# Nine instead of eight fc1 feature tiles run once per batch, in a diffusion transformer block

## The chip, the cores and the metric

The kernel runs on one core of one Trainium2 chip. The metric is the device time of one execution in microseconds (us), as the median of several executions. Every execution whose state is on record was fast, at a granted TensorE clock of 0.99 to 1.0. The rounds of runs were made on different chips, so each kernel is compared with runs of the kernel before from the same round. Times inside one execution are read from the hardware profile and count from the start of its span. Engines are PE (TensorE matmuls), PEld (its weight loads), DVE (VectorE), ACT (ScalarE), POOL (GpSimd) and SP (SyncE, which issues most DMAs here).

## The reference

```python
B, N, D = 2, 256, 1152;  F = 4 * D;  H = 2          # all data bf16
mod = (silu(c) @ w_mod).reshape(B, 6, 1, D)          # shift, scale, gate for both halves
h = layernorm(x) * (1 + scale_a) + shift_a
... attention with two heads of 576, output projection wo ...
x = x + gate_a * a
h2 = layernorm(x) * (1 + scale_m) + shift_m          # the second LayerNorm
m = gelu(h2 @ w_fc1) @ w_fc2                         # fc1: 1152 -> 4608, fc2: 4608 -> 1152
return x + gate_m * m
```

## The kernel before

The argument is about one place, the seam in fc1 between batch 0 and batch 1. fc1 has KF = 36 feature tiles of 128, each summed over KD = 9 tiles of the input, and T = 512 tokens: 256 of batch 0 and 256 of batch 1. A matmul can stream all 512 tokens at once, but batch 1's second LayerNorm ends later than batch 0's. So the first eight feature tiles run twice with 256 tokens, first for batch 0 and then for batch 1, while batch 1's LayerNorm is still finishing. The other 28 tiles run with 512 tokens.

Token tiles 0 and 1 are batch 0's, 2 and 3 batch 1's. The normalized tokens of each are turned by a transposing DMA (`ln2_transpose`) into `hT`, where `ln2_modulate` applies scale and shift in place:

```python
    def ln2_transpose(t):
        nc.sync.dma_start_transpose(hT[:, :, t * P:(t + 1) * P], xn2[t][:])

    def ln2_modulate(b, ks=range(KD)):
        for k in ks:
            h = hT[:, k, b * N:(b + 1) * N]
            if b == 0 or k % 3 == 2:
                nc.scalar.activation(            # batch 1: k = 2, 5, 8 on ACT
                    h, h, ACT.Identity, bias=shift_m[:, k, b:b + 1], scale=scale_m[:, k, b:b + 1],
                )
            else:
                nc.vector.tensor_scalar(...)     # batch 1: k = 0, 1, 3, 4, 6, 7 on DVE
    ...
    ln2_normalize(3, 4 * P)
    ln2_transpose(3)                             # the fourth transpose: the last tile of batch 1
    w_f1[1] = load_panels("w_f1_1", wfc1_v, D)   # fc1's further weights, same DMA queue
    ...
    MSPLIT = 8
    for b in range(B):
        for m0 in range(0, MSPLIT, 2):
            pacc = acc_tile([P, 2, N], "pacc")
            for m in (m0, m0 + 1):
                for k in range(KD):
                    f1_mm(pacc[:, m - m0, :], m, k, b * N, (b + 1) * N)
            if b == 0 and m0 == MSPLIT - 2:
                ln2_modulate(1)                  # ahead of the GELU of tiles 6 and 7
            nc.scalar.activation(gT[:, m0:m0 + 2, b * N:(b + 1) * N], pacc[:], ACT.Gelu_apprx_tanh)
    ...
    for m in range(MSPLIT, KF):                  # 512 tokens from here on
```

At the very start, PE runs warm-up matmuls on zeros while the first weights load. The experiments use them:

```python
    def warm(n, dst):
        for _ in range(n):
            nc.tensor.matmul(dst[:], zeros[:, 0:P], zeros[:], start=True, stop=True)   # 512 columns, bf16
    warm(2, pwarm)
    ...
    warm(18, pwarm)
```

ACT runs the GELUs and the pieces of `ln2_modulate` in the order in which the program issues them.

## Time and profile before

| | |
|---|---|
| time, first three executions | 245.28 us (245.0 to 245.95) |
| span of the profiled execution | 243.1 us |
| PE busy | 237.1 us, 98% |
| fc1 (line 707), PE busy | 71.0 us |
| start of the first fc1 matmul to start of the first fc2 matmul | 70.79 us |

These lines are from the profile page of the kernel before: busy time per engine, the chain that ended last, and the costliest group (operation, shapes, count, busy us, mean ns, then idle time before it).

```profile
PE 237.1 (98%) x1652; PEld 139.4 (57%) x1652; DVE 83.7 (34%) x194; ACT 66.7 (27%) x130; POOL 31.3 (13%) x47
...
PE 93%; DMA 3%; DVE 1%; SPq 0%; ACT 0%; issue 0%; DVEq 0%
...
L707 PE MATMUL pacc<-hT,w_f 128*128 128x512 bf16 (+1 forms) x396 | 71.0, 340 | 0.0
```

PE is the bound, and fc1 seems to have no gap. The chain in order of time says the same about the seam (start us, length us, what):

```profile
98.56 7.86 PE pacc L707 x72
106.42 0.01 issue
106.42 62.93 PE pacc L707 x324
```

The 72 matmuls of batch 0 are followed by the rest with 0.01 us between. This is where a reader can be misled. The ends of matmuls are modelled and overlap the next start, so a matmul held for 0.15 us leaves no idle time. "Perfetto Trace Analysis" of the Trainium skill (Tensor Engine Instruction) says that the end the profiler reports for a matmul is an estimate computed from its size; this trace agrees, since consecutive 256-column matmuls start 0.109 us apart and are each recorded as 0.273 us long. The starts have to be compared. Those of the records around the seam, in us, with the step from the one before:

```
batch 0, tile 7, k = 8    106.147   0.109
batch 1, tile 0, k = 0    106.425   0.278
                 k = 1    106.683   0.258
                 k = 2    106.791   0.108
                 k = 3    106.938   0.147
                 k = 4    107.196   0.258
                 k = 5    107.304   0.108
                 k = 6    107.452   0.148
                 k = 7    107.708   0.256
                 k = 8    107.817   0.109
```

The steps over 0.109 us add up to 0.69 us lost. ACT's and DVE's timelines show what they follow (start us, length us, engine, line, operation, count, idle time before and what ended it):

```profile
106.01 1.58 ACT L595 ACTIVATE hT<-hT,shift_m,scale_m 128x256 bf16<-128x256 bf16 x3 [0.48 <-DMA hT<-xn]
107.50 0.57 ACT L722 ACTIVATE gT<-pacc 128x512 bf16<-128x512 f32 x1
...
106.03 1.63 DVE L599 TENSOR_SCALAR hT<-hT,scale_m,shift_m 128x256 bf16<-128x256 bf16 x6 [3.77 <-DMA hT<-xn]
```

Both engines idle until the transposing DMA lands, at 106.0 us. The six DVE pieces then take 1.63 us, and PE's matmuls follow them one by one.

### The profile page before, as it was taken

The numbers are of one execution on the slowest core, as the hardware profiler recorded it, in microseconds if no ns is written. First come the engines' busy times: TensorE is split into PE (matmuls) and PEld (weight loads), VectorE is DVE, ScalarE is ACT, GpSimd is POOL, SyncE is SP. The second block draws the span as 40 slices with busy tenths as digits, with TensorE's granted clock in tenths as the row PEclk, the third lists the DMA queues.
The fourth block names the chain that finished last, engine by engine and source line by source line (L and its number), as shares of the span: only waits on it lengthen the run. The fifth ranks groups of instructions, "written<-read, shape, count | busy, mean of one in ns | idle before, by whom it ended". The sixth has DMA issues, their size and how long they took to land.

```text
span 243.1 us, 3903 instructions
## 1 busy us (share of the span) xinstructions
PE 237.1 (98%) x1652; PEld 139.4 (57%) x1652; DVE 83.7 (34%) x194; ACT 66.7 (27%) x130; POOL 31.3 (13%) x47
## 2 busy tenths in 40 slices
PE   8899999999999999999999999999999999999994
PEld 2585444465656676978444444444665666656674
DVE  3752462115635676720000019999002000000001
ACT  7632250133614075773322222333000000000000
POOL 1000013000310615200000000000314211111111
PEclk9999999999999999999999999999999999999999
DMA  6999999999999992299999999999891000000000
GB/s 231 328 334 362 370 327 313 363 362 336 374 235 347 342 193 49 49 236 330 326 327 273 246 206 337 327 326 280 240 282 49 16 19 16 16 20 27 22 16 19
DMA packets 70813, 53.89 MB, mean 222 GB/s; under 512 B 18939, under 2 KB 65419, under 8 KB 70795
## 3 DMA queue, kind: packets, MB, share of 16 engines
q1 hardware_dynamic: 70064, 52.43, 74.1%
q0 software_dynamic: 704, 1.20, 1.8%
q8 instruction: 13, 0.21, 0.4%
q14 instruction: 5, 0.04, 0.1%
q10 hardware_dynamic: 27, 0.00, 0.0%
HBM read 48.08 MB, written 1.19 MB: 203 GB/s over the span
## 4 chain that ended last, share of the span: by engine, by line
PE 93%; DMA 3%; DVE 1%; SPq 0%; ACT 0%; issue 0%; DVEq 0%
PE pacc L707 29%; PE pacc L767 29%; PE pacc L612 7%; PE pacc L503 7%; PE pacc L438 7%; PE pk L253 4%; DMA w_scale_a<-in_w_mod_dram 3%; PE pk L282 2%; PE pn L365 1%; PE pa L530 1%; PE ps_s L458 1%; PE pm L221 1%; DVE stats L163 1%; PE pt L231 1%; PE pg L398 0%; SPq L85 0%
## 5 line engine op out<-in xcount | busy, mean ns | idle before, releaser
L707 PE MATMUL pacc<-hT,w_f 128*128 128x512 bf16 (+1 forms) x396 | 71.0, 340 | 0.0
L767 PE MATMUL pacc<-w_f,gT 128*128 128x384 bf16 (+2 forms) x468 | 70.5, 314 | 0.0
L767 PEld LDWEIGHTS <-gT 128*128 128x128 bf16 x468 | 44.3, 98 | 26.3
L707 PEld LDWEIGHTS <-w_f 128*128 128x128 bf16 x396 | 38.7, 98 | 31.9 <-issue 0.7
L429 DVE SCALAR_TENSOR_TENSOR late<-w_gate_mT,late 128x1152 bf16<-128x1152 bf16 x18 | 24.4, 1357 | 38.0 <-DMA w_gate_mT<-in_w_mod_dram 37.4
L773 DVE TENSOR_TENSOR tmp<-pacc,gate 128x384 f32<-128x384 f32 (+2 forms) x13 | 6.8, 526 | 62.6 <-PE pacc L767 50.3
L744 ACT ACTIVATE gT<-pacc 128x512 bf16<-128x512 f32 x28 | 16.7, 597 | 37.7 <-PE pacc L707 37.7
L612 PE MATMUL pacc<-w_o,big 128*128 128x384 bf16 (+2 forms) x117 | 18.1, 314 | 0.0
L503 PE MATMUL pacc<-w_v,hT 128*128 128x384 bf16 x108 | 17.9, 326 | 0.0
L775 POOL TENSOR_TENSOR o_sb<-tmp,x 128x384 bf16<-128x384 f32 (+1 forms) x12 | 11.6, 972 | 47.6 <-DVE tmp L773 47.6
L438 PE MATMUL pacc<-hT,w_q 128*128 128x512 bf16 x81 | 17.7, 379 | 0.0
L612 PEld LDWEIGHTS <-big 128*128 128x128 bf16 x117 | 10.9, 98 | 7.1 <-DVE big L270 0.6
L503 PEld LDWEIGHTS <-hT 128*128 128x128 bf16 x108 | 10.4, 98 | 7.2 <-issue 0.5
L253 PE MATMUL pk<-big,w_k 128*128 128x256 bf16 (+2 forms) x90 | 13.4, 294 | 0.4 <-ACT big L240 0.4
L438 PEld LDWEIGHTS <-w_q 128*128 128x128 bf16 x81 | 7.8, 98 | 9.8 <-DMA w_q<-in_wqkv_dram 0.5
L618 POOL TENSOR_TENSOR x<-tmp,x_sb 128x384 f32<-128x384 f32 (+1 forms) x11 | 9.8, 888 | 17.4 <-DVE tmp L617 10.7
L420 POOL DMA_DIRECT2D gates_dram<-grow x4 | 2.0, 512 | 71.4 <-DVE grow L730 71.4
L253 PEld LDWEIGHTS <-w_k 128*128 128x128 bf16 x90 | 7.5, 97 | 3.4 <-DMA w_k<-in_wqkv_dram 0.3
L146 PE MATMUL pwarm<-zeros 128*128 128x512 bf16 x23 | 7.7, 483 | 1.2 <-DVE eps_t L92 1.2
L617 DVE TENSOR_TENSOR tmp<-pacc,gate 128x384 f32<-128x384 f32 (+2 forms) x13 | 6.7, 525 | 5.4 <-PE pacc L612 5.3
L595 ACT ACTIVATE hT<-hT,shift_m,scale_m 128x256 bf16<-128x256 bf16 x12 | 6.2, 588 | 3.8 <-DVE stats L624 3.3
L240 ACT ACTIVATE big<-pt,scale_a 128x256 bf16<-128x256 bf16 (+1 forms) x12 | 4.6, 434 | 9.3 <-PE pt L231 7.6
(96 smaller groups left out, 146.8 us busy)
## 6 DMA issues: line engine op xcount, KB each, us to landing
w_f<-in_w_fc_dram SPq DMA_DIRECT2D x14, 864.0 KB, 10.9
w_f<-in_w_fc_dram SPq DMA_DIRECT2D x2, 2592.0 KB, 11.8
w_f<-in_w_fc_dram SPq DMA_DIRECT2D x2, 1728.0 KB, 14.9
w_shift_a<-in_w_mod_dram SPq DMA_DIRECT2D x3, 864.0 KB, 11.3
w_q<-in_wqkv_dram SPq DMA_DIRECT2D x3, 864.0 KB, 12.0
w_v<-in_wqkv_dram SPq DMA_DIRECT2D x3, 864.0 KB, 10.5
w_gate_a<-in_w_mod_dram SPq DMA_DIRECT2D x3, 864.0 KB, 9.9
w_o<-in_wo_dram SPq DMA_DIRECT2D x3, 864.0 KB, 13.8
```

The lines of the kernel that those rows point to most:

```text
L146: nc.tensor.matmul(dst[:], zeros[:, 0:P], zeros[:], start=True, stop=True)
L253: nc.tensor.matmul(pk[m][:, c0:c1], w_k[:, k, m * P:(m + 1) * P], hT0[:, k, c0:c1], start=(k == 0 and c0 == 0), stop=(k == KD - 1), skip_g ...
L429: nc.vector.scalar_tensor_tensor(spill, wT[:, j, :], 1.0, s_all[:, b, :], op0=ALU.mult, op1=ALU.mult, accum_out=dst[:, b * KD + j:b * KD + ...
L438: nc.tensor.matmul(pacc[:], w_q[:, k, m * P:(m + 1) * P], hT[:, k, :], start=(k == 0), stop=(k == KD - 1),)
L503: nc.tensor.matmul(pacc[:], hT[:, k, t * P:(t + 1) * P], w_v[:, k, pnl * PW:(pnl + 1) * PW], start=(k == 0), stop=(k == KD - 1),)
L612: nc.tensor.matmul(pacc[:], aT[:, k, t * P:(t + 1) * P], w_o[:, k, c0:c1], start=(k == 0), stop=(k == KD - 1),)
L618: (nc.vector if (t, i) in ((1, 2), (3, 3)) else nc.gpsimd).tensor_tensor(x1[:, t, c0:c1], tmp[:], x_sb[:, t, c0:c1], op=ALU.add)
L707: nc.tensor.matmul(dst, w_f1[m // KD][:, k, ml * P:(ml + 1) * P], hT[:, k, c0:c1], start=(k == 0), stop=(k == KD - 1),)
L744: nc.scalar.activation(gT[:, m, :], pacc[:], ACT.Gelu_apprx_tanh)
L767: nc.tensor.matmul(pacc[:], gT[:, kk, t * P:(t + 1) * P], w_f2[j][:, r, c0 - n * PW:c0 - n * PW + cw], start=(kk == 0), stop=(kk == KF - 1),)
L773: nc.vector.tensor_tensor(tmp[:], pacc[:], gate_m[:, b, c0:c0 + cw], op=ALU.mult)
L775: (nc.vector if last else nc.gpsimd).tensor_tensor(o_sb[:], tmp[:], x1[:, t, c0:c0 + cw], op=ALU.add)
```

## The change

The extra tile of batch 0 gives PE 9 matmuls (0.98 us) more to do before it needs batch 1's data. The first quarter of fc1's weights holds nine tiles, so nothing has to be loaded earlier. This is the whole diff:

```diff
-    MSPLIT = 8
+    MSPLIT = KD
     for b in range(B):
         for m0 in range(0, MSPLIT, 2):
-            pacc = acc_tile([P, 2, N], "pacc")
-            for m in (m0, m0 + 1):
+            ms = range(m0, min(m0 + 2, MSPLIT))
+            pacc = acc_tile([P, len(ms), N], "pacc")
+            for m in ms:
                 for k in range(KD):
                     f1_mm(pacc[:, m - m0, :], m, k, b * N, (b + 1) * N)
-            if b == 0 and m0 == MSPLIT - 2:
+            if b == 0 and ms[-1] == MSPLIT - 1:
                 ln2_modulate(1)
-            nc.scalar.activation(gT[:, m0:m0 + 2, b * N:(b + 1) * N], pacc[:], ACT.Gelu_apprx_tanh)
+            nc.scalar.activation(gT[:, ms[0]:ms[-1] + 1, b * N:(b + 1) * N], pacc[:], ACT.Gelu_apprx_tanh)
```

It has a side effect that the diff hardly shows: the call of `ln2_modulate(1)` moves one group later, so on ACT the GELU of tiles 6 and 7 now comes ahead of the three pieces k = 2, 5, 8.

## The prediction

> **What bounds the kernel now.** TensorE. The page gives PE 237.1 us busy, 98% of a 243.1 us span, at full granted clock; the chain of waits is 93% PE, with fc1 (line 707) 29% and fc2 (line 767) 29%. From the first fc1 matmul (98.40 us) to the end of fc2 (239.66 us) no PE idle time is charged. Only PE time in that stretch counts.
>
> **PE's work.** Feature tile 8 becomes 18 matmuls of 256 columns in place of 9 of 512. In the records, start to start is 109.15 ns for 256 columns and 215.83 ns for 512: 18 x 109.15 - 9 x 215.83 = +22 ns. The nine extra weight loads (98 ns each) still hide behind 109 ns matmuls.
>
> **The intent: the seam between batches.** Batch 1's fc1 needs the second LayerNorm's modulated columns of batch 1. Their transposing DMA lands at 106.01 us; PE issues batch 0's last matmul at 106.15. The modulation runs six pieces on DVE (pitch 0.257 us, from 106.03) and three on ACT (k = 2, 5, 8; pitch 0.50 us, from 106.01). The single matmul records show PE stretched here, though the page calls it busy: batch 1's first nine matmuls start at 106.43, 106.68, 106.79, 106.94, 107.20, 107.30, 107.45, 107.71, 107.82, where 109 ns steps would have put the last at 107.13. PE loses 0.69 us, each time released about 0.055 us after a DVE piece ended. The extra tile of batch 0 gives PE 9 x 0.109 = 0.98 us of work there, enough to hide the DVE pieces: a gain of up to 0.69 us (0.28%).
>
> **What takes it back.** The order listing shows that the three ACT pieces move behind one more GELU, that of tiles 6 and 7, because the call was tied to the last group. A GELU starts 0.42 us after the start of its last matmul, so at 106.57. The next ACT instruction follows 0.49 us later: k = 2 starts at 107.06, k = 5 at 107.56, k = 8 at 108.06, which ends (0.59 us long) at 108.65; its matmul can start at 108.70. PE, unheld, would want it at 107.24 + 8 x 0.109 = 108.11. So about 0.59 us of stall remains, on ACT in place of DVE. Before starts its 90th fc1 matmul at 108.80, after at 108.70: 0.10 us gained, less 0.02 of longer matmuls: -0.08 us in all.
>
> **The rest.** fc1's second quarter is in flight before the seam and nothing waits for it; the first fc2 load still waits for the same last use of the first quarter, and fc2 starts 50 us later. ACT idles over 1.3 us between GELUs, so two more cost nothing. "TensorE: Matmul & The Clock Gate" of the Trainium skill (Part 2) says that matmuls stay in program order and only weight loads are pulled ahead, so PE cannot fill a stall with later matmuls; the stretched starts agree.
>
> **Predicted time:** 245.2 us, range 244.6 to 245.9 (before spread 245.0 to 245.95). Faster by over 2%: 0.005; within 2%: 0.99; slower: 0.005.
>
> **What would show it.** After: k = 0 and 1 of batch 1's first tile unheld, starts at k = 2, 5, 8 held near 107.7, 108.2, 108.7, each just after an ACT piece; DVE pieces unmoved at 106.03; fc2 starting within 0.2 us of 169.35.
>
> **What would make it wrong.** ACT running the pieces earlier (gain up to 0.7 us), a later GELU (loss), or a shift between sessions larger than the effect.

## The result and the profile after

| | before | after |
|---|---|---|
| time, median of six | 245.45 us (244.97 to 246.12) | 246.12 us (245.65 to 246.45) |
| span of the profiled execution | 243.1 us | 244.3 us |
| start of the first fc1 matmul to start of the first fc2 matmul | 70.79 us | 71.64 us |
| issue of the fourth transpose to its landing | 3.26 us | 5.06 us |
| lost at the seam (steps over 0.109 us, added up) | 0.69 us | 1.52 us |

The two profiled spans differ by 1.2 us: 0.85 us of it is fc1, and 0.39 us is that fc1 starts later (98.79 us against 98.40). This start scatters between profiles of either kernel (98.48 us in a second profile of the changed kernel, 98.50 in one of the kernel before), so the duration of fc1 is the cleaner measure of the change.

The ratio is 1.0025, with a 95% interval from 1.0004 to 1.0046. Ratios here and below are the mean time of one kernel's fast runs over that of the other's fast runs of the same rounds, so they are not quite the ratio of the medians. The change is slower by about a quarter of a per cent, and the measured 246.12 us lies above the predicted range.

The lines of the page that answer to those of before:

```profile
PE 237.1 (97%) x1651; PEld 140.5 (57%) x1661; DVE 83.8 (34%) x194; ACT 66.9 (27%) x131; POOL 31.4 (13%) x47
...
PE 80%; SPq 8%; DMA 8%; DVE 2%; issue 1%; ACT 0%; DVEq 0%; ACTq 0%
...
L707 PE MATMUL pacc<-hT,w_f 128*128 128x512 bf16 (+1 forms) x400 | 70.7, 336 | 1.1 <-DVE hT L599 0.8
```

PE's busy time is the same; what is new is 1.1 us of idle time before fc1's matmuls. (Five of the 405 fc1 matmuls lack a record in this trace.) Most of the fall of PE's share of the chain from 93 to 80% has nothing to do with the seam: in this profile the first 33.9 us of the chain run through DMA issues and the load of `w_q`. In a second profile of the same kernel (after_rep) PE has 89%. The chain in order of time, changed kernel:

```profile
102.23 0.82 ACT xn L577
103.06 0.02 issue
103.07 5.06 DMA hT<-xn
...
108.23 0.36 DVE hT L599
108.59 0.04 issue
108.63 9.74 PE pacc L707 x82
```

The chain leaves PE here: it goes through the normalization of the last token tile, its transposing DMA, 5.06 us from issue to landing, and the first DVE piece. The two timelines, changed kernel:

```profile
106.85 0.60 ACT L723 ACTIVATE gT<-pacc 128x512 bf16<-128x512 f32 x1 [0.92 <-PE pacc L707]
108.22 1.58 ACT L595 ACTIVATE hT<-hT,shift_m,scale_m 128x256 bf16<-128x256 bf16 x3 [0.77 <-DMA hT<-xn]
...
108.23 1.63 DVE L599 TENSOR_SCALAR hT<-hT,scale_m,shift_m 128x256 bf16<-128x256 bf16 x6 [5.57 <-DMA hT<-xn]
```

The GELU that was moved ahead of the ACT pieces was over at 107.45, and ACT then idled for 0.77 us. So in this run it was not the order on ACT that held PE. It was the DMA, which nothing in the diff touches.

The records of this DMA say more. It signals its end by sixteen completions. In the kernel before, they come between 105.83 and 105.93 us. In the changed kernel fifteen come between 106.38 and 106.53, and the sixteenth at 108.13. The same stretch, 105.5 to 107 us, shows a packet of another kind among the DMA packets (queue, kind, packets, MB, share). First the kernel before, then the changed one:

```profile
q1 hardware_dynamic: 401, 0.31, 88.2%
```

```profile
q1 hardware_dynamic: 481, 0.24, 77.9%
q8 instruction: 1, 0.02, 3.7%
```

Queue 8 moves 13 packets of 16,384 bytes per execution, in both kernels. In the changed kernel, one of them runs from 106.04 to 106.92 us. Two of the transpose's 32 four-byte packets (two for each completion, which by their number and place they most likely write) start only at 106.91 and 106.92; the other 30 had started by 105.89. In the kernel before, the corresponding packet of queue 8 starts at 110.21 us.

"Runtime: NRT & Kernel Launch" of the Trainium skill (Instruction fetch mechanics) says what such packets are: an engine's program is streamed in blocks of 16 KiB, 256 instructions, fetched by the sequencer over its own DMA queue. The trace agrees for PE: from the first to the last of the 13 packets, 2,958 PE records pass in the kernel before, about 246 per packet.

### The profile page after: what moved, and what is told of

It reads as the page before. It is cut to its first block, busy times and chain, and to the rows that moved or that the text cites. A ratio compares the mean times of both kernels' runs of the same rounds, so it can differ in the third digit from the quotient of the medians.

```text
span 244.3 us, 3912 instructions
## 1 busy us (share of the span) xinstructions
PE 237.1 (97%) x1651; PEld 140.5 (57%) x1661; DVE 83.8 (34%) x194; ACT 66.9 (27%) x131; POOL 31.4 (13%) x47
## 4 chain that ended last, share of the span: by engine, by line
PE 80%; SPq 8%; DMA 8%; DVE 2%; issue 1%; ACT 0%; DVEq 0%; ACTq 0%
PE pacc L768 29%; PE pacc L707 25%; PE pacc L503 7%; PE pacc L438 7%; PE pacc L612 7%; DMA w_q<-in_wqkv_dram 6%; SPq L106 4%; SPq L112 2%; DMA hT<-xn 2%; PE pa L530 1%; PE ps_s L458 1%; PE pn L365 1%; SPq L102 1%; DVE stats L624 1%; PE pg L398 0%
## 5 line engine op out<-in xcount | busy, mean ns | idle before, releaser
L707 PEld LDWEIGHTS <-w_f 128*128 128x128 bf16 x405 | 39.6, 98 | 31.8 <-issue 1.5
L745 ACT ACTIVATE gT<-pacc 128x512 bf16<-128x512 f32 x27 | 16.1, 597 | 36.5 <-PE pacc L707 36.5
L723 ACT ACTIVATE gT<-pacc 128x512 bf16<-128x512 f32 (+1 forms) x10 | 5.3, 552 | 6.7 <-PE pacc L707 6.6
## 6 DMA issues: line engine op xcount, KB each, us to landing
w_f<-in_w_fc_dram SPq DMA_DIRECT2D x2, 2592.0 KB, 11.8
```

The lines of the kernel that those rows point to most:

```text
L707: nc.tensor.matmul(dst, w_f1[m // KD][:, k, ml * P:(ml + 1) * P], hT[:, k, c0:c1], start=(k == 0), stop=(k == KD - 1),)
L745: nc.scalar.activation(gT[:, m, :], pacc[:], ACT.Gelu_apprx_tanh)
```

## Experiments

Three theories: A: the extra 18 instructions of batch 0 let PE's sequencer reach a block boundary before batch 1's waits instead of after them, so the instruction fetch starts about 4 us earlier and hits the tail of the fourth transpose. B: the late landing was chance. C: the order on ACT costs the time.

The summary of all profiles comes first. "Fetch" is the start of the seventh 16 KB packet, "landing" the time from issue to the last completion of the fourth transpose, "lost" what the seam costs PE in steps over 0.109 us, and "fc1" the time from the first fc1 to the first fc2 matmul; all are read from the records, in us. A ratio's interval is about 0.14 to 0.25% to each side, 0.3 to 0.6 us, so the seam is judged by "landing", "lost" and "fc1".

| run | fetch, after the first fc1 matmul | landing | lost | fc1 | time, median | ratio to before |
|---|---|---|---|---|---|---|
| before | 11.81 | 3.26 | 0.69 | 70.79 | 245.45 | 1 |
| before_rep | 12.41 | 3.30 | 0.73 | 70.83 | 244.99 | 0.9993 [0.9977, 1.0009] |
| before_m20 | 12.75 | 3.25 | 0.69 | 70.79 | 244.97 | 0.9995 [0.9980, 1.0009] |
| before_p18 | 5.30 | 4.26 | 1.69 | 71.80 | 245.76 | 1.0029 [1.0016, 1.0043] |
| after | 7.25 | 5.06 | 1.52 | 71.64 | 246.12 | 1.0025 [1.0004, 1.0046] |
| after_rep | 7.24 | 5.06 | 1.52 | 71.65 | 246.27 | 1.0044 [1.0028, 1.0060] |
| after_m27 | 7.21 | 5.04 | 1.49 | 71.62 | 246.20 | 1.0043 [1.0026, 1.0061] |
| after_m27_fix | 7.35 | 5.08 | 1.53 | 71.66 | 245.84 | 1.0036 [1.0015, 1.0057] |
| after_latew | 7.13 | 4.92 | 1.36 | 71.49 | 245.67 | 1.0026 [1.0002, 1.0049] |
| after_latew_fix | 7.11 | 4.89 | 1.33 | 71.46 | 245.85 | 1.0032 [1.0007, 1.0056] |
| after_m20 | 12.16 | 3.25 | 0.46 | 70.59 | 244.94 | 0.9987 [0.9972, 1.0001] |
| after_m20_fix | 12.68 | 3.26 | 0.00 | 70.13 | 244.27 | 0.9962 [0.9947, 0.9977] |
| after_p96_fix | 1.61 | 3.26 | 0.00 | 70.13 | 244.62 | 0.9976 [0.9952, 1.0000] |

The runs of before to which they are compared had a median of 245.0 us for after_rep, after_m27, after_m27_fix and before_p18, of 245.13 us for before_rep and the three m20 runs, and of 245.3 us for after_p96_fix and the two latew runs.

One more count from the records ties the packet to a place in PE's program. When it starts, PE has begun 1,693 to 1,713 of its matmuls and weight loads in the seven profiles with a late landing, and 1,703 in after_p96_fix, although the number of instructions put in front of fc1 differs there by up to 96. In the other five it has begun 1,768 to 1,788. (Up to eleven records are missing in a trace.)

### The same kernels once more

after_rep is the changed kernel, unaltered.

> The changed kernel once more, unaltered. Theory A (instruction fetch): the PE program is fetched in 16 KB packets, and the extra 18 instructions ahead of batch 1's waits let PE's sequencer cross a block boundary before those waits instead of after them, so one fetch packet falls again at 106.0 +- 0.5 us, on the tail of the last transposing DMA, one of whose sixteen completions again comes 1.5 us after the others (near 108.1); time 245.9 to 246.4, 0.2 to 0.35% over before. Theory B (chance): the late landing was an accident of one execution; the landing is back near 3.3 us after issue and the seam looks as predicted, held on ACT, and the time is within 0.1% of before. Theory C (the GELU ahead of the three ACT pieces costs the time) says the time is the same as last time wherever the landing lies.

The fetch came at 7.24 us, the landing at 5.06 us, with fifteen completions by 106.22 us and the sixteenth at 107.82, and the time was 0.44% over before. Theory B falls: two profiles agree within 0.02 us in fetch, landing and fc1. The ratio was somewhat above the expected 0.2 to 0.35%.

before_rep is the kernel before, unaltered.

> The kernel before unaltered, for a second profile and for the noise of a comparison of one kernel with itself: ratio 1.000 +- 0.0015; fetch again near 11.8 us after fc1's start, landing 3.2 to 3.4 us after issue, 0.69 us stretched at the seam.

It came out as expected, and it also shows the noise of such a comparison: 0.07% off one, with an interval of about 0.16% to each side.

### Moving the fetch into the transpose, in the kernel before

```diff
-    warm(18, pwarm)
+    warm(9, pwarm)
+    warm_half(18, pwarm)      # 256 columns each: the same work in 18 more instructions (a matmul and its weight load are two)
```

> The kernel before with 9 of the warm-up matmuls cut in half, so 9 more matmuls and 9 more weight loads (18 rows) ahead of everything else and the same columns. Theory A: the block boundary now lies ahead of batch 1's waits; a fetch packet falls near 104.7 us, amid the last transpose's data, in place of 110.2; that transpose lands 0.8 to 1.6 us later and the kernel is slower by about that much, +0.3 to 0.65%. Theories B and C: no change, within 0.1% of before.

This is the kernel before with eight tiles; only nine warm-up matmuls were cut in half, and they are over at 9.4 us. The fetch moved from 11.8 to 5.3 us after the first fc1 matmul, into the middle of the fourth transpose, which landed 1.0 us later; the kernel became 0.29% slower, just under the range. The DMA packets from 103.5 to 105.5 us, and then the chain of before_p18, in order of time:

```profile
q1 hardware_dynamic: 513, 0.13, 114.5%
q8 instruction: 1, 0.02, 4.1%
```

```profile
102.94 4.26 DMA hT<-xn
...
107.30 0.36 DVE hT L604
107.65 0.04 issue
107.70 62.93 PE pacc L712 x324
```

So the loss can be produced without the change, at the far end of the program. Theory C cannot explain that. Two details differ. Here all sixteen completions were late (107.05 to 107.20), not one. And the packet started 1.95 us before that of the changed kernel, counted from the start of fc1, where 9 matmuls fewer of run-up account for 0.98 us.

### A shift that did not happen

after_m27 was meant to take 27 instructions out of the warm-up.

```diff
-    warm(18, pwarm)
+    warm_f32(9, pwarm)        # fp32, 256 columns
```

> The changed kernel with the 18 bf16 warm-up matmuls at the start written as 9 fp32 ones on the same zeros: PE's instruction stream has 27 rows fewer ahead of everything else, no work in the body differs. Theory A: the block boundary now lies behind batch 1's waits again, the fetch comes after the stall (near 109 to 111 us), the transposing DMA lands 3.3 us after its issue, and what is left is the stall on ACT that the prediction described: matmuls k = 2, 5, 8 held, 0.5 to 0.7 us lost; time 0.5 to 0.8 us under the changed kernel, level with before within 0.1%. Theories B and C: as slow as the changed kernel, +0.2 to 0.3% over before.

On the chip each fp32 matmul ran as two passes, 0.427 us apart at first and 0.215 us apart later, as the bf16 ones of 512 columns do, each with its own weight load, so the number of instructions was unchanged: 1,584 PE records ahead of the first fc1 matmul, as in after_rep. The fetch stayed at 7.21 us, the landing at 5.04 us and the time at 0.43% over before. As a test of theory A it failed; it is a control that the kind of warm-up does not matter.

after_m27_fix has the same warm-up, and the order on ACT as it was in the kernel before:

```diff
-            if b == 0 and ms[-1] == MSPLIT - 1:
+            if b == 0 and m0 == 6:
                 ln2_modulate(1)
```

> The 27 rows fewer, and the second modulation call back ahead of the GELU of tiles 6 and 7, so the three ACT pieces start when the transpose lands. Theory A: both costs gone; nine matmuls of extra work hide all of the modulation, no stall over 0.1 us at the seam, and the time is 0.4 to 0.75 us under before (-0.15 to -0.3%), and 0.4 to 0.6 us under the run with 27 rows fewer alone. Theory C expects the gain over the changed kernel to come from this reordering alone, so after_m27 as slow as the changed kernel and this one fast. Theory B: level with before less 0.6 us at most, with no relation to the fetch.

Because the shift did not happen, this is a test of theory C alone. Restoring the order left the loss at the seam as it was (1.53 us against 1.49) and the time at 0.36% over before. While the transpose lands late, the order on ACT is worth nothing. Theory C falls.

### Moving the fetch out of the transpose, in the changed kernel

```diff
-    warm(18, pwarm)
+    warm_f32(4, pwarm)        # fp32, 512 columns: 16 instructions in place of 36; POOL zeroes an fp32 tile for it
```

> The 27-row shift before did not come about on the chip: an fp32 matmul ran there as two passes, each with its weight load, and the fetch stayed at 7.2 us after the start of fc1. Here 18 bf16 warm-up matmuls become 4 fp32 ones of 512 columns, 16 instructions in place of 36, so 20 rows fewer. Theory A: the block boundary falls behind batch 1's waits, the fetch comes after the stall (10 to 13 us after fc1's start, 11.8 in the kernel before), the fourth transpose lands 3.2 to 3.4 us after its issue, and a stall of 0.5 to 0.7 us is left at the seam, on ACT pieces, as predicted at first; time level with before within 0.15%, 0.6 to 1.0 us under the changed kernel. If the late landing has another cause than the fetch, the time stays 0.4% over before.

The fetch now started at 12.16 us, after the seam, the transpose landed in 3.25 us, and the loss of the changed kernel was gone: 0.13% under before, an interval that just includes no change. The packets from 105.5 to 107 us are of one kind again:

```profile
q1 hardware_dynamic: 470, 0.27, 92.9%
```

What was left at the seam is what the prediction described, a little less of it than expected (0.46 us, against 0.5 to 0.7). The chain of after_m20 (here fc1 is line 713, and its first matmul starts at 98.71 us, 0.32 us later than in the kernel before):

```profile
98.88 9.52 PE pacc L713 x86
108.40 0.00 issue
108.40 0.49 PE pacc L713 x3
108.89 0.00 issue
108.89 8.35 PE pacc L713 x74
```

The held matmuls are k = 2, 5 and 8 of batch 1's first tile, at 107.91, 108.40 and 108.89 us. The ACT and DVE timelines of after_m20 show ACT's three pieces behind the GELU, and no longer idle before them, while DVE started 0.9 us earlier:

```profile
106.77 0.60 ACT L729 ACTIVATE gT<-pacc 128x512 bf16<-128x512 f32 x1 [0.92 <-PE pacc L713]
107.27 1.57 ACT L601 ACTIVATE hT<-hT,shift_m,scale_m 128x256 bf16<-128x256 bf16 x3
...
106.33 1.63 DVE L605 TENSOR_SCALAR hT<-hT,scale_m,shift_m 128x256 bf16<-128x256 bf16 x6 [3.76 <-DMA hT<-xn]
```

after_m20_fix also restores the order on ACT, by the same edit as above.

> The same with the second modulation call back ahead of the GELU of tiles 6 and 7. Theory A: no stall over 0.15 us at the seam; 0.4 to 0.75 us faster than before (-0.15 to -0.3%) and 0.4 to 0.7 us faster than the run with 20 rows fewer alone. If the landing stays late, it is level with the changed kernel, as the same reordering was without the shift.

It is the fastest kernel: 0.38% under before, and 0.25% under after_m20 (0.9962 against 0.9987, both to the same runs of before). The 0.38% is more than was expected (0.15 to 0.3%) and more than fc1 explains (0.66 us shorter, 0.27%); the interval, 0.23 to 0.53%, covers the difference. No matmul at the seam is held, and the chain runs through it in one piece:

```profile
99.02 17.90 PE pacc L713 x163
```

before_m20 is the control, the kernel before with the same edit of the warm-up.

> Control: the kernel before with the same 20 rows fewer in the warm-up. Its boundary lies behind the waits already, so all theories expect no change: within 0.15% of before, the fourth transpose landing 3.2 to 3.4 us after issue, 0.69 us stretched at the seam. A difference here is what the edit of the warm-up itself does.

No change, as expected: fetch after the seam, 0.69 us lost, ratio 0.9995. The gains of the two runs above do not come from the warm-up itself.

### The other way

If it is the place of the fetch that counts, more instructions must help as well as fewer, provided the fetch is over before the fourth transpose starts.

```diff
-    warm(18, pwarm)
+    warm(2, pwarm)
+    warm_quarter(64, pwarm)   # 128 columns each: 96 instructions more
-            if b == 0 and ms[-1] == MSPLIT - 1:
+            if b == 0 and m0 == 6:
```

> The shift the other way: 16 of the 18 warm-up matmuls cut into 64 quarters of 128 columns, 96 rows more at the top, with the modulation call back ahead of the GELU of tiles 6 and 7. If it is the place of the fetch that matters and not the number of rows, the fetch now falls well ahead of the last two transposes (0 to 3 us after fc1's start), the fourth transpose lands 3.2 to 3.4 us after issue with all sixteen completions together, no stall over 0.15 us at the seam, and the time is 0.5 to 1.0 us under before, as with 20 rows fewer. If fewer rows were what helped, it is level with the changed kernel or slower. The finer warm-up may itself cost or save up to 0.3 us at the start.

The fetch moved to 1.61 us after the first fc1 matmul. That is not ahead of the last two transposes, as expected, but only of the fourth: it runs from 101.28 to 102.43 us, beside the first 1.15 us of the third, which still lands in 3.19 us, as in before (3.20). The landing of the fourth is back at 3.26 us, the seam loses nothing, and fc1 takes the same 70.13 us as in after_m20_fix. The time is 0.24% under before, with an interval that just reaches no change, and less under it than with 20 instructions fewer: in its profile fc1 starts at 99.66 us, 0.8 us later than in after_m20_fix. That the finer warm-up costs this time at the start is likely, but no run shows it.

### Is it the queue behind the fetch?

In the changed kernel the sixteenth completion came 1.2 us after the fetch packet ended. Weight packets for fc1's second quarter stood in the same DMA queue behind the transpose. after_latew holds them back by a tiny store that waits for the GELU of tiles 4 and 5:

```diff
+            if b == 0 and m0 == 4:
+                nc.sync.dma_start(scr[:], gT[0:1, m0, 0:8])
+                ... the loads of w_f1[1] to w_f1[3] and what followed them, moved here ...
```

> The changed kernel with the fetch left where it is, but the weight loads behind the last transpose held back: a tiny store on their queue waits for the GELU of tiles 4 and 5 first. This asks how much of the 1.6 us by which one completion is late is the 0.9 us fetch itself, and how much is the weight packets queued behind it. If the queue matters, the last completion comes 0.4 to 0.7 us after the fetch packet ends (1.2 before), 4.3 to 4.6 us after the transpose's issue, and the time is 0.4 to 0.8 us under the changed kernel. If only the fetch matters, it lands 5.0 to 5.1 us after issue as before and the time is unchanged. The later weight loads themselves should cost nothing: they are first used 11 us later.

The first weight packet now came at 107.06 us instead of 105.4 (after_rep), and between 105.5 and 107 us the DMA queues held almost nothing but the fetch. These are the packets of that stretch in after_latew:

```profile
q8 instruction: 1, 0.02, 3.7%
q1 hardware_dynamic: 17, 0.00, 1.3%
```

The sixteenth completion still came at 107.72 us, 4.92 us after issue, 1.18 us after the fetch packet ended at 106.54. My guess falls: the weights behind it explain 0.15 us of the delay. The time, 0.26% over before, is not clearly different from the changed kernel.

after_latew_fix adds the restored order on ACT.

> The same with the modulation call back ahead of the GELU of tiles 6 and 7. With the landing at 4.3 to 4.6 us after issue it removes what is then held on ACT: up to 0.3 us under after_latew. With the landing still at 5.1 us, no change.

With the landing at 4.89 us it changed nothing (fc1 71.46 us against 71.49), as the second branch of the expectation said.

## Why the prediction was wrong

**The step that failed** is the premise in "The intent: the seam between batches" and "DVE pieces unmoved at 106.03": that the transposing DMA lands where it did before, because the diff does not touch it. It landed 1.8 us later after its issue (5.06 us against 3.26). The list of what would make it wrong did not have that either. The sum fits: with the later landing the seam of the kernel before would have lost 0.69 + 1.80 = 2.49 us; the extra tile hides 0.98 us of it, which leaves 1.51, and 1.52 us were measured. Against the 0.69 us of before that is a loss of 0.83 us, and fc1 took 0.85 us longer.

**What was right.** PE bounds the kernel, and in fc1 outside the seam nothing moved: 0.02 us of the 0.85 us is left for the nine weight loads and shorter matmuls, as predicted. The remaining stall on ACT was right in mechanism and nearly in size: 0.46 us in after_m20 against 0.59 predicted. Most of the difference is one term of the sum: the GELU started 0.31 us after the start of its last matmul, not 0.42. The starts of k = 2, 5, 8, less the 0.32 us by which that fc1 began later, are 107.59, 108.08 and 108.57, against 107.7, 108.2 and 108.7. The gain from moving the pieces back (up to 0.69 us against before) was also there once the landing was: fc1 in after_m20_fix is 0.66 us shorter than before. But these were true of a kernel with the fetch elsewhere, not of the one that was asked about.

**What is shown, and what is argued.** It is shown that the late landing goes with the place of the fetch packet. In the seven profiles where the packet starts 5.3 to 7.4 us after the first fc1 matmul the landing takes 4.26 to 5.08 us; in the six where it starts at 1.6 or after 11.8 us it takes 3.25 to 3.30 us. Edits of the warm-up, which do no work for the result, bring the late landing about in the kernel before and take it away from the changed one. Why the fetch moves by some 4.5 us is an inference that fits all runs. If PE's program is fetched ahead and PE cannot run past the matmuls that wait for `hT`, the first of those is the place to look at. Counting PE's matmuls and weight loads from the start, it is row 1,722 in the kernel before and row 1,740 in the changed one (1,576 rows ahead of fc1 in after_rep, two for each of 81 matmuls, its own weight load and itself). If the block boundary lies between those rows, the fetch comes before the stall in one and after it in the other. By the same count, before_p18 has that matmul at 1,740, after_m20 at 1,720 and before_m20 at 1,702, and each fell on the side that this says. That the packet starts near the same row of PE's program in eight profiles, and some 70 rows later in the five where the waits come first, agrees with it.

**What stays open.** The trace does not tell which DMA engine a packet ran on, so that the fetch and the last completion shared one is inferred from the times. Nor is it shown from which moment of a transpose on a fetch beside it costs time. In twelve of the profiles the sixth packet overlaps the first 1.2 us of the second transpose at most, which lands in 3.17 to 3.27 us, so the beginning seems to be harmless; in before_p18 a packet from 1.02 us after the issue on was not. And a fetch is not the only thing that makes a transpose late: the first of the four takes 4.12 us in the kernel before, though the packet near it starts only 3.59 us after its issue. The 1.2 us from the fetch's end to the last completion is not explained by weights in the queue. "DMA: Bandwidth & Descriptors" of the Trainium skill (Queues, rings and completion order) says that the semaphore write of a DMA lands only after every earlier write of that DMA engine, across its queues. That would make the completion wait for the fetched block to be written. after_latew agrees with it, but no run shows it. Why before_p18's packet was 1 us earlier than 9 matmuls account for, and why all sixteen completions were late there, is open too.

## What to carry to other kernels

A change of 0.7 us has to be checked for what it does to the place of instruction fetches: inserting or removing instructions ahead can move a 16 KB DMA packet (18 more moved it by 4.6 us here), and if it falls on the later part of a DMA that the critical path waits for, it can turn a gain into a loss. When a wait got longer on something the diff does not touch, look at its single completions, and test by shifting the program with idle instructions before believing or dropping the change. And tie a call to the data it needs, not to "the last group" of a loop: here the second modulation slid behind a GELU, which cost 0.46 us once the landing was early.

## What the Trainium skill lacked or had wrong

- "Runtime: NRT & Kernel Launch" (Instruction fetch mechanics) calls the cost of crossing a 16 KiB boundary mostly hidden. Here the packet took 0.88 us (1.31 us in before_p18), and one beside the tail of a transposing DMA went with a landing of 5.06 us in place of 3.26 and fc1 0.85 us longer. The page does not warn of that.
- No page was found that says when PE's fetch starts relative to matmuls held on a semaphore. Here 18 instructions more ahead of the held ones moved it from 11.8 to 7.2 us after the first fc1 matmul.
- "FP8 and Floating Point Precision" counts four passes for a true fp32 matmul. The time here agrees (two passes of 0.215 us per 256 columns, against 0.109 us for bf16), but the instructions do not: the trace has two matmuls, each with its own weight load, per fp32 matmul, and each takes 0.427 us per 256 columns at the start and 0.215 us later, as long as 512 bf16 columns. This matters for counting instructions.
- "Perfetto Trace Analysis" (Tensor Engine Instruction) says that a matmul's end is an estimate, but not that stalls vanish by it: 0.69 us of held matmuls at the seam of the kernel before appear as 0.0 us of idle time.
